# A third order of TensorE groups and loads, from a planner with a new model of the load queue

## The chip, the core and the metric

The kernel runs on one core of a Trainium2 chip. The metric is device time in microseconds (us), of which six runs were taken: the median is 226.64 us, the lowest 226.03 us and the highest 227.13 us. One further execution was profiled. Everything said below of durations and waits comes from that one execution.

## What is computed

The reference is a streaming attention (a window of 128 keys and four sink keys), followed by a dense feed-forward stage with a gated activation:

```python
def _attn_ref(q, k, v, n_sink, window):          # q, k, v: (4, 8, 768, 64)
    scores = np.matmul(q, k.transpose(0, 1, 3, 2)) / np.sqrt(D)
    pos = np.arange(S)
    rel = pos[:, None] - pos[None, :]
    keep = (pos[None, :] < n_sink) | ((rel >= 0) & (rel < window))
    a = softmax(np.where(keep, scores, -1e9))    # over the keys
    return np.matmul(a, v)

def _moe_ref(x, w_in, w_out, beta):              # x: (3072, 512), w_in: (512, 2048)
    h = x @ w_in
    g = h * (1.0 / (1.0 + np.exp(-beta * h)))
    return g @ w_out                             # (3072, 512)
```

The softmax is written out with a maximum and an epsilon in the original; `x` is the attention's output with its heads put side by side. The inputs and the output are float32.

## The kernel before

**Tiles.** The 3072 tokens are cut into eight blocks of 384 tokens (`hb` 0 to 7), two to a batch element. Within a block the eight heads go in four pairs (`hp`), so there are 32 attention units. For each block the kernel loads q, k and v, casts them to bf16, brings q and k into transposed form, makes the scores of a unit in two groups of small matmuls, takes the exponential on ScalarE, masks the result, multiplies it with v, divides, transposes back into `xT`, and runs the feed-forward stage: 16 slices `m` of `w_in` (four matmuls of 384 columns each), an activation on ScalarE and a multiplication on VectorE for each, and then `w_out` (four times four matmuls of 512 columns for each of three row tiles).

**Groups.** TensorE's work is cut into groups, each with a letter. `T` transposes q and k of one head pair (blocks 0 and 1; L697, six matmuls). `C` and `D` are the two score groups of a unit (L783); they use 64 rows of the array at a time. `S` is the score against the sink keys (L819). `A` is the product with v (L861 and L851). `X` transposes the attention output of blocks 0 and 1 (L880). `h` and `g` are the first and second half of one `w_in` slice of blocks 0 and 1, `H` the whole slice of a later block (L910). `O` is a quarter of an output tile (L931). `b` brings in `beta`. Blocks 2 to 7 are transposed by DMA instead of by `T` and `X` (`XT`, L734, and `XO`, L891).

**What sets the order.** The string `ORDER`, one letter for a group, is TensorE's order, written out as data. The planner in `Graph.schedule` walks through it and places the work of all engines in estimated time, one instruction at a time: it picks for each operation one of the engines that can do it (a cast can go to VectorE, ScalarE or GpSimd), and thereby fixes the order on every engine's queue, including SyncE's queue of DMA issues. On the chip each queue then runs strictly in that order, with semaphores for the dependences. `PAR['l0']` is the order of the eleven loads of block 0, and `PAR['mix']` says how the loads of blocks 1 and 2 (`a`) and of the sixteen weight pieces (`w`) are interleaved. All loads form one chain on SyncE in that order.

**The planner's model.** `Graph.place` estimates when a DMA is issued and when it lands. `Graph.fillers` puts matmuls on a constant tile (`ones`, at most 512 columns, in steps of 128) into gaps in which the planner expects TensorE to wait, up to 48 us of planned time and only while a PSUM bank is free; they compute nothing that is used (L1027). Eight PSUM banks hold all matmul results; a `C` or `D` group takes two, every other group one, until the engine that reads them is done.

**Lines that matter below.** L563 and L558 are casts and copies on VectorE and ScalarE, L560 casts on GpSimd; L792 the exponential; L798, L803 and L809 the masks; L823 the exponential of the sink scores; L866 and L868 the division; L915 and L917 the activation's two steps; L635, L647 and L940 the loads of q, k, v, the loads of weights, and the stores of the output.

Of the kernel before, what the change touches and what calls it, by code (L numbers as in the profile page):

```python
# [11 lines left out]
DM, DF, NOUT = 512, 2048, 512  # L12
# [10 lines left out]
PAR = {'MD': 1, 'XB': 2, 'l0': [0, 2, 6, 1, 3, 4, 9, 5, 7, 10, 8], 'mix': 'aawwaawawawwawwaaaawwawwawwwawaa'}  # L23
ORDER = ('TCDTSTTDCSDSCASCTADACbXXAhhhXXThghDghgDhggThgggChhgghgShDSghSghghTghgCASCAXADOXOAhhhhXOXOgOOggOOhghg'
         'hhgOOOghgghghhhghgOgOSDgSChCOghSgADODCCOODOOSAAOAOSSOCCSOSODCHHHHHHHHOHDDOHAHDCHHAHHHAAOODDOOOODCDOH'
         'SCCHHOOASSHHOHOHHHHHSHHHAACSHSOHDCCOAODDOOCCDOAOOHHSHSAOHHOHAAHHHHHHHSHOHOHOSSOCDOHDCCOHHAOOHHHHHSHH'
         'HOSOCCDOHHOHODDAHOAHAOODCCASOOOCDDHHHHHHOAOHOOSHHOOSAHHAOHHHHHOOOHHHHOOHHHHHHOOHHHHOHOOOOOHOOOOOOOOO'
# [10 lines left out]
class Op:  # L38
    __slots__ = ("eng", "fn", "deps", "signal", "count", "waits", "sem", "vc", "dma", "seq", "end", "ns", "alts",
                 "group", "tail", "preds", "left", "succ", "at", "queue", "ring", "lag", "x", "tag", "chain")  # L40
# [6 lines left out]
class Graph:  # L47
# [4 lines left out]
    LEAD, PAD, LATE = 1500, 2000, 90000  # L52
    BIAS, EARLY = 300, 100000
    FILL_TO = 48000
    RING, FETCH, SWITCH = 165, 900, 85
    DEPTH = 9

    def __init__(self):
        self.ops = []
        self.groups = []  # L60
        self.writers = {}
        self.readers = {}
        self.last_load = None
        self.filler = None
# [7 lines left out]
    def add(self, eng, fn, ns=0, r=(), w=(), x=(), dma=None, alts=None, queue=470, ring=64, lag=0, after=(), tag=None):  # L72
# [4 lines left out]
        o.queue, o.ring, o.lag, o.x, o.tag, o.chain = queue, ring, lag, list(x), tag, None  # L77
# [28 lines left out]
    def place(self, o, at):  # L106
        o.at = at
        if o.dma:
            self.pending = [x for x in self.pending if x[0] > at]
            issued, need = at + o.queue + 40, min(o.ring, self.RING)  # L110
            total = sum(n for _, n in self.pending)
            for f, n in self.pending:
                if total + need <= self.RING:
                    break
                issued, total = max(issued, f), total - n
            begin = issued + o.lag if o.lag else at + 1150 + o.ns
            self.dma_free = max(self.dma_free + o.ns, begin)
            self.pending.append((self.dma_free, o.ring))
            self.free[o.eng] = issued
            o.end = self.dma_free + 950 + (self.PAD if at > self.LATE else 0)  # L120
# [942 lines left out]
```

The softmax here doesn't subtract the row's maximum and nothing guards it: scores larger than these inputs give would overflow.

## Time and profile before

| what | value |
|---|---|
| median of six runs | 226.64 us |
| time of the profiled execution | 226.55 us |
| its span, first to last instruction | 224.8 us |
| TensorE (PE) busy | 217.7 us, 97% of the span |
| VectorE (DVE) and ScalarE (ACT) busy | 141.5 us each, 63% |
| GpSimd (POOL) busy | 66.2 us, 29% |
| DMA moved | 40.95 MB, 182 GB/s on average |
| fillers on PE (L1027) | 31 matmuls, 10.6 us busy |
| last instruction of PE ends | 221.94 us |

The span lies 1.75 us below the time of its own execution; this constant part lies around the kernel's instructions. In the first slices of the page PE is between 70% and 90% busy, and from 20 us on practically all the time. Matmuls overlap in the pipeline, so the busy time of a single one (371 ns on average at L931) is longer than the distance from one to the next (0.216 us for 512 columns, read from four in a row that take 0.86 us in the chain of waits). When work is added up for PE, that distance is the right measure.

### The profile page before, as it was taken

Reading aid. Unit: us, or ns where it says so; the run is one execution under the profiler, and the core shown is the slowest. Engines: PE = TensorE matmul, PEld = TensorE weight load, DVE = VectorE, ACT = ScalarE, POOL = GpSimd, SP = SyncE. Lnnn points to the kernel's source line nnn. Section 1 sums busy time; section 2 is a strip of 40 time slices with the busy share of each in tenths; the row PEclk is TensorE's granted clock in tenths of the full one; section 3 lists DMA queues with packets and bytes.
Section 4 is the critical chain, followed back from the end, with each engine's and each line's share of the span. In section 5 each row is a group of like instructions: output and inputs, shape, how many; then the busy total and the mean of one; then the engine's idle time right before and its main releaser. Section 6 shows DMA issues by size and latency. Waiting matters only on the chain.

```text
span 224.8 us, 4484 instructions
## 1 busy us (share of the span) xinstructions
PE 217.7 (97%) x1720; PEld 119.5 (53%) x1720; DVE 141.5 (63%) x313; ACT 141.5 (63%) x257; POOL 66.2 (29%) x157
## 2 busy tenths in 40 slices
PE   8978999999999999999999999999999999999994
PEld 2545555555455546545554665455455556555443
DVE  1798999778757278839775578657362626455100
ACT  2595998134882867547788847778757756566221
POOL 7274345000362626352109510241435400000000
PEclk9999999999999999999999999999999999999999
DMA  7999989997999999999999999993133033101112
GB/s 158 268 332 372 358 217 322 350 253 136 220 224 206 217 208 234 183 255 219 207 241 186 210 219 221 248 252 104 47 85 82 0 85 83 47 4 47 47 47 93
DMA packets 104741, 40.95 MB, mean 182 GB/s; under 512 B 93312, under 2 KB 97680, under 8 KB 104720
## 3 DMA queue, kind: packets, MB, share of 16 engines
q1 hardware_dynamic: 103152, 40.65, 79.6%
q8 instruction: 13, 0.21, 0.5%
q10 hardware_dynamic: 1568, 0.02, 0.4%
q14 instruction: 8, 0.07, 0.1%
HBM read 27.30 MB, written 6.29 MB: 149 GB/s over the span
## 4 chain that ended last, share of the span: by engine, by line
PE 71%; DVE 12%; DMA 7%; SPq 6%; ACT 2%; issue 1%
PE P L931 32%; PE P L910 28%; DMA v_stage<-in_v_dram 5%; SPq L635 4%; DVE g L917 4%; PE P L861 4%; PE P L783 3%; DMA k_stage<-in_k_dram 3%; DVE k L563 1%; PE P L851 1%; DVE onorm L868 1%; SPq L891 1%; DVE E L809 1%; PE P L819 1%; DVE vaug L563 1%; DVE w_in L563 1%
## 5 line engine op out<-in xcount | busy, mean ns | idle before, releaser
L931 PE MATMUL P<-w_out,g 128*128 128x512 bf16 (+2 forms) x400 | 93.1, 371 | 0.1
L910 PE MATMUL P<-xT,w_in 128*128 128x384 bf16 x512 | 92.7, 326 | 0.0
L915 ACT ACTIVATE t<-P,hbeta 128x384 f32<-128x384 f32 x128 | 71.8, 586 | 31.4 <-PE P L910 24.1
L917 DVE SCALAR_TENSOR_TENSOR g<-t,P 128x384 bf16<-128x384 f32 x128 | 68.0, 549 | 35.5 <-ACT t L915 32.8
L798 POOL TENSOR_SCALAR_AFFINE_SELECT E<-E 128x256 bf16<-128x256 bf16 (+1 forms) x109 | 52.2, 510 | 58.0 <-ACT E L792 57.9
L910 PEld LDWEIGHTS P<-xT,w_in 128*128 128x128 bf16 x512 | 48.4, 98 | 34.7 <-issue 0.8
L931 PEld LDWEIGHTS P<-w_out,g 128*128 128x128 bf16 x400 | 36.6, 98 | 37.1 <-issue 1.1
L792 ACT ACTIVATE E<-P 128x768 bf16<-128x768 f32 (+1 forms) x64 | 45.6, 760 | 14.2 <-PE P L783 14.0
L861 PE MATMUL P<-vaug,E 128*128 128x65 bf16 x352 | 18.6, 193 | 0.8 <-DVE E L803 0.5
L558 ACT ACTIVATE osb<-P 128x512 f32<-128x512 f32 (+2 forms) x16 | 9.1, 571 | 15.4 <-PE P L931 15.1
L861 PEld LDWEIGHTS P<-vaug,E 128*128 128x128 bf16 x352 | 16.5, 97 | 4.1 <-ACT E L792 0.7
L868 DVE TENSOR_TENSOR onorm<-P,rden 128x384 bf16<-128x384 f32 x32 | 17.4, 553 | 0.5
L783 PE MATMUL P<-qkT 64*128 64x128 bf16 (+1 forms) x256 | 16.4, 239 | 1.0 <-ACT E L792 0.4
L823 ACT ACTIVATE ES<-P 128x128 bf16<-128x128 f32 (+1 forms) x32 | 12.1, 391 | 7.0 <-PE P L819 7.0
L563 DVE CAST k<-k_stage 128x512 bf16<-128x512 f32 (+1 forms) x24 | 11.8, 490 | 5.4 <-DMA k_stage<-in_k_dram 5.2
L783 PEld LDWEIGHTS P<-qkT 64*128 64x128 bf16 x256 | 8.2, 94 | 12.2 <-issue 4.3
L851 PE MATMUL P<-vS,ES 128*128 128x130 bf16 x64 | 12.7, 221 | 0.9 <-DVE vS L686 0.6
L563 DVE CAST q<-q_stage 128x512 bf16<-128x512 f32 (+1 forms) x19 | 9.2, 483 | 6.8 <-DMA q_stage<-in_q_dram 6.7
L563 DVE CAST vaug<-v_stage 128x512 bf16<-128x512 f32 x18 | 7.9, 438 | 7.8 <-DMA v_stage<-in_v_dram 7.7
L725 POOL TENSOR_TENSOR kS<-qkT,headm 128x8 bf16<-128x8 bf16 x16 | 3.0, 209 | 32.4 <-DMA qkT<-k 28.8
L1027 PE MATMUL P<-ones 128*128 128x512 bf16 (+2 forms) x31 | 10.6, 473 | 1.2 <-POOL ones L569 1.1
L809 DVE TENSOR_TENSOR E<-E,maskS 128x512 bf16<-128x512 bf16 x16 | 8.5, 532 | 3.4 <-ACT E L792 3.2
(48 smaller groups left out, 88.3 us busy)
## 6 DMA issues: line engine op xcount, KB each, us to landing
v_stage<-in_v_dram SPq DMA_DIRECT2D x24, 256.0 KB, 4.8
out_dram<-osb SPq DMA_DIRECT2D x23, 256.0 KB, 2.6
q_stage<-in_q_dram SPq DMA_DIRECT2D x18, 256.0 KB, 4.7
k_stage<-in_k_dram SPq DMA_DIRECT2D x18, 256.0 KB, 5.7
wst<-in_moe_w_in_dram SPq DMA_DIRECT2D x5, 512.0 KB, 7.9
wst<-in_moe_w_out_dram SPq DMA_DIRECT2D x4, 512.0 KB, 7.7
g<-in_moe_w_out_dram SPq DMA_DIRECT2D x4, 512.0 KB, 7.6
q_stage<-in_q_dram SPq DMA_DIRECT2D x8, 192.0 KB, 4.6
```

What stands on the lines that cost most here:

```text
L563: return lambda e: e.tensor_copy(dst, at())
L783: add("pe", lambda e, dst=dst, own=own, kc=kc, rows=rows, q0=q0, nq=nq: e.matmul(dst(), tokens(own, hp, 1, rows, kc, 1)[:, 0, :], tokens(h ...
L792: add("act", lambda e, src=src, dst_=dst_: e.activation(dst_, src(), AF.Exp, bias=0.0, scale=SCALE), act_ns(256 * n), w=[(k_, z, j) for k_ ...
L798: alts = {"gp": (lambda e, d=d, sg=sg, at_=at_: e.affine_select(d, d, [[0, 2 * len(at_)], [sg, 128]], ALU.is_ge, 0.0, base=min(sg, 0), cha ...
L823: add("act", lambda e: e.activation(ES[z][:, q0:q1], P[:, bs[0], q0:q1], AF.Exp, bias=0.0, scale=SCALE), act_ns(q1 - q0), w=[("ES", z)], x ...
L851: add("pe", lambda e, m=m, o0=o0: e.matmul(A()[:, o0:o0 + 2 * (D + 1)], ES[z][:, (c0 + m) * 128:(c0 + m + 1) * 128], vS[b % 2][:, 2 * hp:2 ...
L861: e.matmul(A()[:, o0:o0 + D + 1], E[z][:, i, hh, :], vaug[vz][:, kb % NK, 2 * hp + hh, :], start=a, stop=o, skip_group_check=True), 39,
L868: add("dve", lambda e: e.tensor_tensor(onorm[:, on, 2 * c0:2 * c1, :], av()[:, :, 0:D], rden[on][:, 0:2 * nb].unsqueeze(2).to_broadcast([1 ...
L910: first = add("pe", lambda e, c=c: e.matmul(hp(), w_in16[:, c, m * 128:(m + 1) * 128], xT[:, hb, c, 128 * c0:128 * c1], start=(c == 0), st ...
L915: add("act", lambda e: e.activation(tt[ti][:, 0:n], hp(), AF.Tanh, bias=0.0, scale=hbeta[:, m:m + 1]), act_ns(n) + 93, r=["hbeta"], w=[("t ...
L917: add("dve", lambda e: e.scalar_tensor_tensor(gt[hb % NG][:, m, 128 * c0:128 * c1], tt[ti][:, 0:n], 1.0, hp(), ALU.add, ALU.mult), dve_ns( ...
L931: add("pe", lambda e, m=m: e.matmul(P[:, bk[0], a:b], gt[hb % NG][:, m, t * 128:(t + 1) * 128], w_out16[:, m, a:b], start=(m == 0), stop=( ...
```

## The change

The change replaces the two data strings and the model behind them. The matmuls of the kernel's own work, their shapes and their number stay the same, as do the loads and stores.

```diff
-PAR = {'MD': 1, 'XB': 2, 'l0': [0, 2, 6, 1, 3, 4, 9, 5, 7, 10, 8], 'mix': 'aawwaawawawwawwaaaawwawwawwwawaa'}
-ORDER = ('TCDTSTTDCSDSCASCTADACbXXAhhhXXThghDghgDhggThgggChhgghgShDSghSghghTghgCASCAXADOXOAhhhhXOXOgOOggOOhghg'
+PAR = {'MD': 1, 'XB': 2, 'l0': [2, 3, 1, 6, 9, 0, 7, 8, 5, 4, 10], 'mix': 'waawwaawawaaawwwaaawwawwwwaaawaw'}
+ORDER = ('TTSDCSTDCCTAASCDDTXbSAXCDAXShhhXhThgghggghhTgCDTgghhhggghShhCghgggDSDAAASChXgOXOXAOhXhhhgghggOgOhgOO'
...
-    LEAD, PAD, LATE = 1500, 2000, 90000
-    BIAS, EARLY = 300, 100000
-    RING, FETCH, SWITCH = 165, 900, 85
+    LEAD, PAD, LATE = 2000, 2000, 90000
+    BIAS, EARLY = 400, 45000
+    FETCH, SHORT, SWITCH = 1150, 400, 85
+    SMALL = {"sp": (42, 80), "dve": (50, 180), "gp": (56,), "act": (193,)}
+    DMA = {"nat": ((434, 580, 580, 580, 470), 64, 1140, 115, 2250), "hb": ((434, 580, 580, 580, 470), 64, 2290, 115, 3390),
...
+    FETCHES = (152, 232, 368, 477, 608, 730, 858, 988, 1111, 1222, 1354, 1482, 1601, 1728)
...
-            begin = issued + o.lag if o.lag else at + 1150 + o.ns
-            self.dma_free = max(self.dma_free + o.ns, begin)
-            self.pending.append((self.dma_free, o.ring))
-            self.free[o.eng] = issued
-            o.end = self.dma_free + 950 + (self.PAD if at > self.LATE else 0)
+            prev, start = self.last_dma
+            issued = max(at + quick[prev], wait, start + 2370 if prev == 2 else 0)
...
+            f = max(self.dma_free + svc, at + 3090 if kind == "xt" else issued + lag)
...
+            self.pending.append((max(self.dma_free, f - svc), f, n + 1, o))
+            self.dma_free = f
+            self.free[e] = issued + 43
+            o.end = f + 600 + (self.PAD if at > self.LATE else 0)
...
+        if rows:
+            t -= self.SWITCH
...
-            n = min(512, int((t - now) * 2.4 / slow) // 128 * 128)
+            room = t - now - (self.SWITCH if self.rows else 0)
+            n = min(512, int(room * 2.4 / slow) // 128 * 128)
```

What it does to the model: each kind of DMA has its own issue time, service time and lag (`DMA`); the fetches of program code are charged to the load queue at listed places (`FETCHES`, `SMALL`); masks on VectorE are charged more (for instance 430 instead of 335 ns for the sink mask), and a matmul of 65 columns less (36 instead of 39 ns); ScalarE is charged a handicap of 400 instead of 300 ns against VectorE, but only up to 45 us instead of 100 us; fillers leave room for the change of the array's row mode before and after score groups. There is also a new option to issue output stores from ScalarE, which is not switched on.

What it does to the program, read from the built instruction streams: PE has 1738 matmuls instead of 1720, and all 18 more are fillers. The leading run of fillers is 25 of 512 columns and one of 384, instead of 12 and one. All fillers together have 22016 columns instead of 15104. Up to the first `O` group both programs hold the same work of PE. The sequence of PE changes into or out of score groups (64-row mode) 64 times instead of 74 times; from the first `O` on, 44 instead of 46 times. The loads of block 0 come in the order q1, k1, k0, q3, v1, q0, k3, v0, k2, q2, v2 instead of q0, q1, q3, k0, k1, q2, v1, k2, k3, v2, v0 (q and k by head pair, v by token tile). Before the first activation product (L917) VectorE has 13 casts of q and k and 4 copies of `T` results instead of 10 and 2; ScalarE has no such casts and 2 copies instead of 3 and 4.

## The prediction, made before the changed kernel ran

> **What bounds the kernel now.** I read the page's engine table first (PE busy 97%), then PE's timeline, which splits the run into two stages.
>
> ```profile
> PE 217.7 (97%) x1720; PEld 119.5 (53%) x1720; DVE 141.5 (63%) x313; ACT 141.5 (63%) x257; POOL 66.2 (29%) x157
> ```
>
> ```profile
> 1.06 5.62 PE L1027 MATMUL P<-ones 128*128 128x512 bf16 x13 [1.06 <-POOL ones L569]
> 6.47 0.45 PE L697 MATMUL P<-ident,q 128*128 128x128 bf16 x3
> ...
> 19.79 1.14 PE L910 MATMUL P<-xT,w_in 128*128 128x384 bf16 x6
> ...
> 38.10 1.03 PE L931 MATMUL P<-w_out,g 128*128 128x512 bf16 x4
> ...
> 84.31 0.34 PE L783 MATMUL P<-qkT 64*128 64x256 bf16 x3 [0.31 <-DVE g L917]
> ...
> 213.10 8.84 PE L931 MATMUL P<-w_out,g 128*128 128x512 bf16 x56
> ```
>
> Start, duration, what, count, and in brackets the idle time and its releaser. Up to 38.1 us PE is busy largely with fillers; from the first O group (L931, 38.10) to its end at 221.94 it streams. Does PE's content explain that stage? Distances between matmuls, from rows in a row: 0.1625 us (384 columns), 0.216 (512), 0.0295 (L861), 0.057 (L851), 0.0545 and 0.030 (score matmuls of 256 and 128 columns), 0.056 (transposes), 0.11 for each change into or out of score groups. Over all counts of the page this gives 197.9 us of own work: L910 83.2, L931 83.0, L861 10.4, L851 3.6, L783 10.0, L819 3.5, the rest 4.2. Before the first O lie 20.4 us of it, after it 177.5. So 177.5 + 46 x 0.11 = 182.5, against 221.94 - 38.10 = 183.8 measured: only **1.3 us** of stalls are left there. The two largest are the waits near 73.3 (for a DMA transpose of k) and 82 to 84 us (banks held by L917).
>
> What bounds the first stage is in the chain of waits:
>
> ```profile
> 6.59 5.77 DMA v_stage<-in_v_dram
> 12.38 0.43 DVE vaug L563
> ...
> 23.69 0.48 ACT t L915
> 24.20 0.56 DVE g L917
> 24.75 0.48 DVE k L563
> ```
>
> Loads until 12.4 us, then mostly VectorE one instruction after another, until 35 us. VectorE's own timeline shows its last steps before the O stage, and ends with the second w_out cast, which the first O group needs:
>
> ```profile
> 22.95 0.56 DVE L917 SCALAR_TENSOR_TENSOR g<-t,P 128x384 bf16<-128x384 f32 x1 [0.86 <-ACT t L915]
> ...
> 37.60 0.78 DVE L563 CAST w_out<-g 128x1024 bf16<-128x1024 f32 x1
> ```
>
> So the end is (first O group) + 182.5 + stalls + 2.9 us of tail (224.8 - 221.94). A changed order can win at the O group's time, at the changes of row mode, and at 1.3 us of stalls.
>
> **The change part by part.**
>
> *First transposes.* VectorE's first casts, each waiting for its load, begin at 3.84, 4.96, 5.75 and 6.35; ScalarE's (the sixth load) at 7.63, the v load after it at 8.77. A pair load thus adds 0.6 us and a v load 1.14. In the new order T0 and T1 need q0, now sixth behind a v load: 6.35 + 1.14 + 0.6 = 8.1, with a cast of 0.42 about 8.55. The leading fillers are 25.75 units of 512 columns. The row above has 13 in 5.62 us, 0.43 each, twice the later 0.216: a slow clock until about 6.2 us, though the page's granted-clock row shows 9 throughout. Twelve at 0.43 and 13.75 at 0.216 end at 9.15.
> A rule speaks against so many fillers. The Trainium skill, "TensorE: Matmul & The Clock Gate", Part 1, says the slow clock lasts about 3.4 us of sustained activity, and returns only after an idle window as long; waiting PE needs no matmuls for shorter gaps. By it, 8 fillers at 0.43 and 17.75 at 0.216 end at 8.3, and T0 would start with its data at 8.55, 0.6 us earlier. The trace shows 5.1 us, and fast matmuls after unfilled gaps of up to 0.61 us. I take the row, 9.15, against 6.47 before; but T1 follows at once (before: 8.79), and all four T's need loads that land by 11.1 in both.
>
> *From there to the first activation product.* VectorE's order with its steps (cast 0.42, T copy 0.86, v cast 0.35, vS 0.36, sink mask 0.3 to 0.57, other mask 0.2, onorm 0.46, rden 0.1): T0's copy 9.65 to 10.5; v0, k2, vS, q2 until 12.05; so T2 at 12.1 and, after vS and a mask, its copy until 13.5; C2 at 13.6, T3 until 14.2, masks of units 0 and 1 until 14.85, T3's copy until 15.7, C3 then; q and k of block 1, onorm 0 and 1 with masks until 18.8, onorm 2 19.6, onorm 3 20.9 (before 20.3), the last two xT copies and a T copy until 22.7. The first whole w_in slice ends on PE at 22.5, ScalarE takes 0.57, the first L917 begins at about **23.3** (before 22.95). By then VectorE has done 1.9 us more than before: 3 casts 1.25, 2 T copies 1.7, a mask 0.2, less a v cast, an xT copy and a weight cast 1.2. It had 1.9 us of waits for loads and ScalarE after 9 us (brackets 0.16, 0.48, 0.44, 0.86) to put it in. The 13.5 extra filler units (2.9 us) lie in PE's waits here and cost nothing while VectorE is last; without that cover each could hold a ready group by 0.2 us.
>
> *From there to the first O.* After the first L917 up to the same w_out cast VectorE does, new: 13 L917 6.0, 6 weight casts 3.6, 3 casts 1.25, a T copy 0.86, 2 v casts 0.7, 3 rden and an onorm 0.75: 13.2. Before: one T copy and one xT copy more, a rden less: 14.2, which took 14.9 (23.4 to 38.3). In that ratio 13.8 us: 23.8 + 13.8 = 37.6 for the cast's end, and O 0.2 ahead of it as before (its first two matmuls don't need this cast): 37.4. But each L917 also waits for its L915, and ScalarE's 16 of them with the exponentials between take 13.5 us from 22.7. Between 37.4 and 38.1 (nothing won) I take **37.9**, near the row of before. The w_out load is no nearer bound: the same loads stand before it on SyncE, and it lands ahead of its cast. Ends: 37.2 (the sum, and ScalarE early), and 39.4 if the 1.9 us find no gaps.
>
> *Steady stage.* Own work the same, two changes of mode less: -0.2. The stalls: the bank wait at 82 to 84 is tied to the old order; nine w_in slices in a row (36 matmuls) follow three score groups there now, and ScalarE, at 0.47 a slice against PE's 0.65, catches up. The other, the transpose of block 3's k: its third cast at VectorE now stands behind the sink mask of unit 3, whose score group is at 68.6; exponentials until 70.2, mask and cast until 71.1, transpose 3.7 more (as in the old issue at 69.48 that PE got at 73.2): 74.8, needed at 74.5. A wait of 0.3, as now. On SyncE an output store and one `XO` stand ahead of it (0.9 and 1.24 us), but their inputs are ready by 68. Behind it wait all of PE. Stalls **1.3 as before**; ends 0.4, since two gaps go, and 3.0, since a planner's miss anywhere here is paid in full.
>
> *Model constants, fillers' room, unused store option:* no instruction of their own; they act through the orders just counted. The tail keeps its last instructions and stays 2.9.
>
> Sum on the profile: -0.2 (first O) - 0.2 (modes) + 0 (stalls) = -0.4: span 224.4, execution 226.15. The profiled execution lies 0.1 below the median; -0.4 on the median gives **226.2 us**.
>
> **The rivals.**
> *The order recovers more: 224.7.* If PE only lost what no order can avoid, it would run from 9.15 through 197.9 + 64 x 0.11 + 17.25 fillers of 0.216 = 208.7, to 217.8, 4.1 us before the old end. VectorE's chain forbids most of it. But first O at 37.2 (-0.9), -0.2, and stalls at 0.5 (-0.8) make -1.9. For it: ScalarE is freed of three casts and two T copies ahead of the activations, and the longer fillers say that the new model expects these waits. Against: VectorE is what bounds, and gets more.
> *The late start is not won back: 227.7.* The mechanism is VectorE's queue between 9 and 23 us. T0 is 2.7 us later, and the 1.9 us of added casts and copies come behind it; a single exponential or mask later than I put it leaves VectorE idle, in order. If none of the gaps is filled, the first L917 begins at 22.95 + 1.9 = 24.8, 1.5 later than in the sum; O at 39.4, and -0.4 + 1.5 = +1.1 gives 227.7. It makes the kernel slower from a first L917 at 23.7 on, measurably from 24.4. For it: T2 and T3 both wait for VectorE here. Against: the loads land as early as before.
> *The order is changed but the time is not:* within the main case.
>
> **How the numbers follow.** What a measurement of this kernel can tell from no change is 0.3%, 0.68 us, so 225.96 to 227.32. Main case 226.2, own range 225.2 to 227.2, chance 0.40: 0.17 below the band, 0.19 in it, 0.04 above (its open ends of stalls). Recovery 224.7 (224.0 to 225.5): 0.23, all faster. Late start 227.7 (227.0 to 230, where new stalls come on top): 0.37, of it 0.05 in the band. Faster 0.40, same 0.24, slower 0.36. The range leaves out the far ends of both rivals: 224.5 to 228.6.
>
> **What would show it.** PE's timeline: first transposes at 9.15 (8.6 if the rule holds), first O near 37.9, last PE end near 221.5. VectorE's: first L917 at 23.3, hardly idle after it. The wait before L783 near 74.5 at 0.3 or less. I am wrong if first O lies outside 37.2 to 38.6, or if waits of more than 2 us in all appear on PE after it, whatever the total.

## The result, and the profile after

The changed kernel takes 227.84 us (median of 36 runs, 227.44 to 229.61), the kernel before, in 73 runs beside it, 226.80 us (226.03 to 228.71). The ratio is 1.0048 with an interval of 1.0038 to 1.0059: the change costs about 1.1 us. (The profiled execution of after took 227.51 us, that of before 226.55.) The forecast was 226.2, a small gain. The measured value lies outside the main case's own range (225.2 to 227.2) and inside the wide one that took in the rivals (224.5 to 228.6), 0.14 us from the rival "late start not won back" (227.7).

The engine line of the page after, then TensorE's timeline with the lines that answer to those shown of before:

```profile
PE 218.2 (97%) x1738; PEld 120.3 (53%) x1738; DVE 138.6 (61%) x311; ACT 141.0 (62%) x259; POOL 69.4 (31%) x157
```

```profile
1.06 7.71 PE L1070 MATMUL P<-ones 128*128 128x512 bf16 x26 [1.06 <-POOL ones L610]
8.60 0.33 PE L738 MATMUL P<-ident,q 128*128 128x128 bf16 x3
...
21.23 1.15 PE L951 MATMUL P<-xT,w_in 128*128 128x384 bf16 x6
...
39.17 0.59 PE L972 MATMUL P<-w_out,g 128*128 128x512 bf16 x2
39.96 0.61 PE L972 MATMUL P<-w_out,g 128*128 128x512 bf16 x2 [0.19 <-DVE w_out L604]
...
77.03 0.67 PE L824 MATMUL P<-qkT 64*128 64x256 bf16 x12 [0.68 <-DMA qkT<-k]
...
211.43 11.43 PE L972 MATMUL P<-w_out,g 128*128 128x512 bf16 x68
```

All lines of the code stand 41 further down than before, or a little more (L910 is now L951, L931 L972, L917 L958). The first O group starts at 39.17, before at 38.10: 1.07 us later. TensorE ends at 222.86, before at 221.94: 0.92 later. So from the first O on, the new program needs 183.69 us where the old one needed 183.84. **The loss is made in the first 39 us**, and the later stage is level. In after only two matmuls of the first O group stand ahead of a wait for the second `w_out` cast, so the third one is followed below as well: 39.96 against 38.53 in before.

Who bounds these 39 us is in the chain of waits (start, duration, what):

```profile
6.54 4.58 DMA q_stage<-in_q_dram
...
11.14 0.42 DVE q L604
...
17.41 0.43 DVE E L850
17.84 1.05 DVE E L844
18.89 0.47 DVE onorm L909
19.36 0.10 DVE rden L907
19.46 0.84 DVE E L844
20.30 0.48 DVE onorm L909
20.78 0.05 issue
20.83 0.34 PE P L921 x3
```

From the landing of the tenth load (q2, 11.12) to the third transposition of the attention output (20.83) there is nothing in the chain but VectorE. Two masks (L844) take 1.05 and 0.84 us of it. VectorE's timeline around them, and below it GpSimd's:

```profile
17.77 1.12 DVE L844 TENSOR_TENSOR E<-E,maskT 128x256 bf16<-128x256 bf16 x1
...
19.39 0.92 DVE L844 TENSOR_TENSOR E<-E,maskT 128x256 bf16<-128x256 bf16 x1
20.22 0.55 DVE L909 TENSOR_TENSOR onorm<-P,rden 128x384 bf16<-128x384 f32 x1
20.69 0.41 DVE L604 CAST q<-q_stage 128x384 bf16<-128x384 f32 x1
...
21.48 0.55 DVE L909 TENSOR_TENSOR onorm<-P,rden 128x384 bf16<-128x384 f32 x1
...
24.57 1.02 DVE L958 SCALAR_TENSOR_TENSOR g<-t,P 128x384 bf16<-128x384 f32 x2
```

```profile
17.53 1.22 POOL L601 TENSOR_SCALAR_AFFINE_SELECT w_in<-wst 128x1024 bf16<-128x1024 f32 x1
18.71 0.45 POOL L839 TENSOR_SCALAR_AFFINE_SELECT E<-E 128x256 bf16<-128x256 bf16 x1
19.12 1.04 POOL L601 TENSOR_SCALAR_AFFINE_SELECT w_in<-wst 128x1024 bf16<-128x1024 f32 x1
```

Two masks of the same line in before, with GpSimd's cast that runs beside the second one:

```profile
16.87 0.24 DVE L803 TENSOR_TENSOR E<-E,maskT 128x256 bf16<-128x256 bf16 x1
...
17.61 1.04 DVE L803 TENSOR_TENSOR E<-E,maskT 128x256 bf16<-128x256 bf16 x1
```

```profile
17.47 1.05 POOL L560 TENSOR_SCALAR_AFFINE_SELECT w_in<-wst 128x1024 bf16<-128x1024 f32 x1
```

In before such a mask took 0.24 and 0.28 us, and once 1.04. In after two start while GpSimd casts a weight, and end just after that cast does. The last division of block 0 (L909 at 21.48) stood at 19.79 before: **1.69 us later**. From it on, both programs take the same way: transposition, copy to `xT`, second half of a `w_in` slice, L956, L958. That took 3.16 us before (19.79 to 22.95) and 3.09 now (21.48 to 24.57). From the first L958 to the third O matmul it is 15.4 us, before 15.6. So 1.43 of the division's 1.69 us arrive at the third O matmul.

### The profile page after: what moved, and what is told of

The parts are those of the page before. It is cut to its first block, busy times and chain, and to the rows that moved or that the text cites. A ratio compares the mean times of both kernels' runs of the same rounds, so it can differ in the third digit from the quotient of the medians.

```text
span 225.7 us, 4514 instructions
## 1 busy us (share of the span) xinstructions
PE 218.2 (97%) x1738; PEld 120.3 (53%) x1738; DVE 138.6 (61%) x311; ACT 141.0 (62%) x259; POOL 69.4 (31%) x157
## 4 chain that ended last, share of the span: by engine, by line
PE 84%; DVE 6%; DMA 4%; SPq 2%; ACT 1%; issue 0%
PE P L951 36%; PE P L972 36%; PE P L824 5%; PE P L902 4%; SPq L676 2%; DMA q_stage<-in_q_dram 2%; DMA qkT<-k 2%; PE P L892 1%; PE P L860 1%; DVE E L844 1%; DVE onorm L909 1%; DVE g L958 1%; DVE qkT L604 1%; DVE E L850 1%; DVE w_out L604 1%; ACT E L833 1%
## 5 line engine op out<-in xcount | busy, mean ns | idle before, releaser
L958 DVE SCALAR_TENSOR_TENSOR g<-t,P 128x384 bf16<-128x384 f32 x128 | 68.0, 548 | 43.4 <-ACT t L956 40.8
L956 ACT ACTIVATE t<-P,hbeta 128x384 f32<-128x384 f32 x128 | 71.3, 585 | 36.4 <-PE P L951 30.0
L951 PE MATMUL P<-xT,w_in 128*128 128x384 bf16 x512 | 94.0, 326 | 0.0
L972 PE MATMUL P<-w_out,g 128*128 128x512 bf16 (+2 forms) x400 | 92.2, 371 | 0.2 <-DVE w_out L604 0.2
L839 POOL TENSOR_SCALAR_AFFINE_SELECT E<-E 128x512 bf16<-128x512 bf16 (+1 forms) x108 | 54.0, 527 | 84.9 <-ACT E L833 84.3
L951 PEld LDWEIGHTS P<-xT,w_in 128*128 128x128 bf16 x512 | 47.6, 98 | 33.7 <-issue 0.8
L972 PEld LDWEIGHTS P<-w_out,g 128*128 128x128 bf16 x400 | 37.1, 98 | 38.1 <-issue 0.9
L599 ACT ACTIVATE osb<-P 128x512 f32<-128x512 f32 (+2 forms) x24 | 14.0, 584 | 17.2 <-PE P L972 17.1
L604 DVE CAST q<-q_stage 128x512 bf16<-128x512 f32 (+1 forms) x25 | 12.0, 482 | 10.0 <-DMA q_stage<-in_q_dram 9.9
L824 PE MATMUL P<-qkT 64*128 64x128 bf16 (+1 forms) x256 | 15.7, 239 | 2.4 <-ACT E L833 1.0
L909 DVE TENSOR_TENSOR onorm<-P,rden 128x384 bf16<-128x384 f32 x32 | 17.5, 551 | 0.5
L1070 PE MATMUL P<-ones 128*128 128x512 bf16 (+3 forms) x49 | 13.1, 402 | 1.1 <-POOL ones L610 1.1
L604 DVE CAST k<-k_stage 128x512 bf16<-128x512 f32 (+1 forms) x25 | 11.2, 450 | 3.7 <-DMA k_stage<-in_k_dram 3.6
L850 DVE TENSOR_TENSOR E<-E,maskS 128x512 bf16<-128x512 bf16 x16 | 7.4, 465 | 6.5 <-ACT E L833 6.1
```

What stands on the lines that cost most here:

```text
L599: return lambda e: e.activation(dst, at(), AF.Copy, bias=0.0, scale=scale)
L604: return lambda e: e.tensor_copy(dst, at())
L824: add("pe", lambda e, dst=dst, own=own, kc=kc, rows=rows, q0=q0, nq=nq: e.matmul(dst(), tokens(own, hp, 1, rows, kc, 1)[:, 0, :], tokens(h ...
L839: alts = {"gp": (lambda e, d=d, sg=sg, at_=at_: e.affine_select(d, d, [[0, 2 * len(at_)], [sg, 128]], ALU.is_ge, 0.0, base=min(sg, 0), cha ...
L909: add("dve", lambda e: e.tensor_tensor(onorm[:, on, 2 * c0:2 * c1, :], av()[:, :, 0:D], rden[on][:, 0:2 * nb].unsqueeze(2).to_broadcast([1 ...
L951: first = add("pe", lambda e, c=c: e.matmul(hp(), w_in16[:, c, m * 128:(m + 1) * 128], xT[:, hb, c, 128 * c0:128 * c1], start=(c == 0), st ...
```

## The experiments

All kernels but two keep the planner's finished plan and move single instructions in it: `find(G, key, engine)` names an instruction by what it writes, `move(G, o, engine, x)` puts it on that engine's queue ahead of `x`. Each was timed in five rounds beside the kernel before, in six groups with their own times of before (226.64 to 227.47 by the medians), so the ratio is what compares them. The ratios have intervals of 0.1% to 0.3% to either side, so a single step of 0.3 us is not told apart by a time; the profile of each says where it went. A profile is one execution, and can lie off its kernel's median (b1's by 1.2 us).

| program | time, us | ratio to before (interval) | last division | first L917 / L958 | third O matmul | from there to PE's end |
|---|---|---|---|---|---|---|
| before | 226.80 | 1 | 19.79 | 22.95 | 38.53 | 183.4 |
| after | 227.84 | 1.0048 (1.0038–1.0059) | 21.48 | 24.57 | 39.96 | 182.9 |
| e1_hold_pool | 228.62 | 1.0050 (1.0029–1.0071) | 20.82 | 24.40 | 39.97 | 184.0 |
| e3_casts_act | 227.95 | 1.0029 (1.0010–1.0048) | 21.09 | 24.22 | 39.84 | 183.3 |
| e5_q0_early | 228.28 | 1.0040 (1.0019–1.0061) | 21.58 | 24.67 | 40.29 | 184.1 |
| e7_k_first | 228.48 | 1.0050 (1.0029–1.0071) | 21.73 | 24.82 | 40.44 | 182.8 |
| e2_masks_pool | 227.59 | 1.0029 (1.0014–1.0045) | 20.52 | 24.11 | 39.45 | 183.4 |
| e6_wout_early | 227.81 | 1.0048 (1.0031–1.0064) | 21.42 | 24.51 | 39.81 | 182.3 |
| e8_k2_early | 228.28 | 1.0052 (1.0035–1.0070) | 22.11 | 25.47 | 40.59 | 183.2 |
| e10_before_load | 227.41 | 1.0030 (1.0015–1.0045) | 20.59 | 23.22 | 38.81 | 183.4 |
| g1_old_front | 228.05 | 1.0047 (1.0033–1.0062) | 19.70 | 22.79 | 38.59 | 185.2 |
| g2_old_front_mask | 227.67 | 1.0028 (1.0013–1.0042) | 18.84 | 21.82 | 37.63 | 184.7 |
| f1_light_dve | 227.68 | 1.0037 (1.0017–1.0057) | 20.89 | 24.84 | 40.30 | 183.4 |
| e4_no_late_fill | 228.44 | 1.0088 (1.0060–1.0115) | 21.40 | 24.47 | 40.02 | 183.2 |
| a1_short_lead | 228.13 | 1.0055 (1.0034–1.0077) | 21.39 | 24.47 | 39.87 | 183.8 |
| f2_light_short | 227.09 | 1.0019 (0.9999–1.0040) | 20.20 | 24.14 | 39.39 | 183.2 |
| b1_before_mask | 226.60 | 0.9996 (0.9978–1.0015) | 18.73 | 22.51 | 38.15 | 185.1 |
| f3_front | 227.05 | 0.9996 (0.9975–1.0017) | 20.16 | 23.38 | 38.98 | 184.2 |
| a2_k6_early | 228.47 | 1.0072 (1.0046–1.0099) | 21.82 | 24.91 | 40.31 | 182.8 |
| f4_front_k6 | 226.57 | 0.9987 (0.9971–1.0003) | 20.14 | 23.37 | 38.76 | 183.6 |

### Is it the masks beside GpSimd, VectorE's work, or the late start?

**e1_hold_pool**: GpSimd's second weight cast waits until VectorE's last mask is done.

```diff
+m = find(G, ("p", 3, 1), "dve")
+w, nxt = find(G, ("w16", 0, 1)), find(G, ("w16", 1, 0))
+move(G, w, "gp", nxt)
+w.deps.append((m, False))
```

> The changed kernel's plan with one edit: GpSimd's second w_in cast comes after its last mask of unit 3 and waits for VectorE's mask of that unit, so that neither of VectorE's two masks at 17.8 and 19.4 us has a GpSimd weight cast beside it; no engine gets more or less work. Collision theory (the masks last 1.12 and 0.92 us instead of 0.25 because of those casts, and everything on VectorE behind them is late): the masks fall to 0.25 to 0.45, first L958 product from 24.57 to about 23.3, first O group from 39.2 to about 38.2, total 0.8 to 1.4 us below the changed kernel (226.4 to 227.0), level with the kernel before. Added-work theory (VectorE is late because it got casts and copies): at most 0.3 us. Late-start theory (the first transposes begin 2.1 us later and that is what shows at the end): no gain.

The masks fell to 0.48 and 0.24 us and the last division came 0.66 earlier. But the cast, now at 19.17, met a cast of VectorE instead: the q cast at 19.49 took 1.00 us. Another, at 23.57, took 0.91 beside GpSimd's third weight cast, which it just misses in after. The first L958 gained 0.17 only, and the ratio did not fall. Moving GpSimd's cast moved the collision.

**e3_casts_act**: the casts of block 1's first q and k on ScalarE.

```diff
+es = [o for o in G.ops if ("ES", 2) in o.keys][0]
+for n in "qk":
+    move(G, find(G, (n + "16", 1, 0, 0), "dve"), "act", es)
```

> The changed kernel's plan with the two casts of block 1's first q and k (VectorE at 15.1 and 15.9 us, 1.2 us together) moved to ScalarE, where they stand ahead of the sink exponential of unit 2 in a gap at 14.4 us. Added-work theory: VectorE's chain is 1.1 to 1.2 us shorter, first L958 about 23.5, total 0.8 to 1.2 us lower. Collision theory: the same 1.2 us are taken out of the chain ahead of the masks, but the masks then wait for exponentials of ScalarE and still meet the weight casts, so 0.2 to 0.6 us. Late-start theory: no gain.

The division came 0.39 earlier, the first L958 0.35, though the first transposes were 0.5 later (9.12) in this execution; the ratio fell by 0.0019, with an interval that overlaps after's. The two masks, now earlier against GpSimd's casts, took only 0.34 and 0.38 us, but the q cast behind them took 1.15 (19.61) beside the next weight cast (19.44 to 20.48): here too the collision moved.

**e2_masks_pool**: the two masks on GpSimd, ahead of its weight cast.

```diff
+for o in (find(G, ("d", 2, 1), "dve"), find(G, ("p", 3, 1), "dve")):
+    o.eng = "gp"
+    o.fn, o.ns = o.alts["gp"]
+move(G, find(G, ("w16", 0, 1)), "gp", find(G, ("w16", 1, 0)))
```

> After, with the two masks of VectorE that GpSimd's weight casts stretched (17.77 us, 1.12 us long; 19.39 us, 0.92 us long) done on GpSimd ahead of its second weight cast; all else in its place. VectorE loses 2.0 us of its queue ahead of the first L958 (0.5 us of it work, 1.5 us stretch). If VectorE's queue between 11 and 23 us sets the first activation product, the first w_in matmul comes 1.0 to 2.0 us earlier than 21.23, the first L958 at 23.0 to 23.8 (after: 24.57), the third O matmul at 38.6 to 39.2 (after: 39.96), and the time falls by 0.8 to 1.3 us, to about that of the kernel before. If the loss sits behind the first L958 (the bank wait at 28.6, the w_out casts), the first L958 moves but the third O matmul stays within 0.3 us of 39.96, and the time within 0.3 us of after's.

The division moved by 0.96 us. The first L958 kept 0.46 of it, and it, the third O matmul and the time all fell short of what was expected. VectorE's timeline and GpSimd's show why:

```profile
23.26 0.92 DVE L637 CAST q<-q_stage 128x384 bf16<-128x384 f32 x1
24.11 1.00 DVE L991 SCALAR_TENSOR_TENSOR g<-t,P 128x384 bf16<-128x384 f32 x2
```

```profile
22.86 1.04 POOL L634 TENSOR_SCALAR_AFFINE_SELECT w_in<-g 128x1024 bf16<-128x1024 f32 x1
```

A cast of 0.41 us, standing right ahead of the first activation product, met GpSimd's third weight cast.

**e5_q0_early**: q0 loaded fourth, and 8 of the 26 leading fillers left out, so that TensorE starts 1.4 us sooner (7.21).

```diff
+q3, q0 = find(G, ("stg", "q", 0, 3)), find(G, ("stg", "q", 0, 0))
+move(G, q0, "sp", q3)
+move(G, find(G, ("q16", 0, 0, 0)), "dve", find(G, ("q16", 0, 3, 0)))
...
+for o in lead[-9:-1]:
+    G.ops.remove(o)
```

> The changed kernel's plan with q0 loaded fourth instead of sixth (and cast in that order), and eight fillers of 512 columns fewer in the leading run, so that the first transposes begin at about 6.8 instead of 8.6 us. Late-start theory: most of the 1.8 us comes through, total 1.0 to 1.7 us lower. VectorE-chain theories (collision and added work): the chain starts at the cast of q2, whose load lands at 11.1 us either way, so first L958 and the total stay within 0.3 us of the changed kernel.

The last division stayed (21.58), and so did all behind it. The late first transposes are not the cause; the chain begins with q2's load, as the chain of waits says.

**e10_before_load**: the kernel before with more on VectorE.

```diff
+for key in (("qkT", 0, 3, 0, 0), ("q16", 1, 1, 0), ("k16", 1, 1, 0)):
+    o = find(G, key, "act")
+    o.eng = "dve"
+    o.fn, o.ns = o.alts["dve"]
```

> The kernel before with 1.75 us of ScalarE's work ahead of the first activation product given to VectorE, in place: one copy of transposes (0.93 us) and the casts of q and k of one head pair of block 1 (0.41 each). Nothing else of the change: old loads, old TensorE order, old fillers, early start. If VectorE's added work alone makes the loss, the first L917 moves from 22.95 to 24.0 to 24.7, the first O from 38.1 to 38.8 to 39.3, and the time rises by 0.7 to 1.2 us, as the whole change did (1.1). If the loss needs the new order of groups or the later start, the added work goes into VectorE's gaps (0.48 at 12.4, 0.44 at 20.8, 0.86 at 22.9) and the time stays within 0.3 us.

The division was 0.80 late, yet the first L917 only 0.27. VectorE's timeline:

```profile
20.59 0.54 DVE L901 TENSOR_TENSOR onorm<-P,rden 128x384 bf16<-128x384 f32 x1
21.06 0.68 DVE L596 CAST w_in<-wst 128x1024 bf16<-128x1024 f32 x1
21.66 0.34 DVE L596 COPY xT<-P 128x384 bf16<-128x384 bf16 x1
...
23.22 0.55 DVE L950 SCALAR_TENSOR_TENSOR g<-t,P 128x384 bf16<-128x384 f32 x1 [0.89 <-ACT t L948]
```

In before the `w_in` cast behind the division waited 0.44 us for its load (20.79), and the copy of `xT` waits behind that cast. The added work used up this slack first. So before has slack behind its last division that after lacks. The time rose by 0.3%, less than the whole change; it lies between the two expectations.

### Is it TensorE's order behind the first product?

**e6_wout_early** and **e8_k2_early**.

```diff
+move(G, c0, "dve", r0)      # w_out casts ahead of block 1's reciprocals
+move(G, c1, "dve", r1)
```

> After, with the two VectorE casts of the first w_out slices ahead of the reciprocals and divisions of block 1 that wait for TensorE (after: casts at 37.66 and 39.23, their loads land at 34.16 and 36.45). If the late casts set the third O matmul, it starts at 39.4 to 39.6 without a wait (after: 39.96 with waits of 0.2 to 0.3), and the time falls by 0.3 to 0.4 us. If TensorE's own order bounds this stretch, O's two waits vanish but others appear for the divisions (L921, L951 of block 1), and the time stays within 0.15 us. Of the 1.07 us by which the first O is late, neither takes away more than 0.4.

The wait of the third O matmul vanished, but it started 0.15 earlier only, and the ratio stayed at 1.0048.

```diff
+for o in fill:              # the two fillers at 26.03
+    G.ops.remove(o)
+move(G, k2, "dve", g0)      # k cast of 26.11 ahead of the first L958
```

> After, with the cast of block 1's third k (VectorE, 26.11 us, behind a weight cast) moved ahead of the first L958, and without the two fillers at 26.03 that stand in front of the transposes which wait for it. If the path goes from that cast over the transposes, ScalarE's copy of them and the exponential to the second score group of block 1 (28.56 us, 1.0 us of wait), then this group comes at 28.1 to 28.2, the third O matmul at 39.5 to 39.6, and the time falls by 0.4 us although the first L958 is itself 0.3 to 0.4 later. If what bounds is the row of activation products themselves, everything after the first L958 slips with it: the time rises by 0.2 to 0.4 us.

The second score group came 4.26 us after ScalarE's first L956 (24.58; after 4.61), but the third O matmul still came 15.1 us behind the first L958 (after 15.4), which had slipped. In this profile the row of activation products carries the delay on; the ratio, 1.0052, doesn't decide between the two expectations.

**g1_old_front** and **g2_old_front_mask** do not plan; they replay a list: before's instructions up to the first O group on all engines, then after's. g2 also gives before's one stretched mask to GpSimd.

```diff
-        while at_pe < len(todo) or pool:
+        for step in PLAN:
```

> The kernel before up to its first O group, instruction for instruction on every engine (loads, fillers, casts, groups), and behind it after's order of what is left, its casts and stores too. If the whole loss sits ahead of the first O and the changed steady stage is itself worth 0.2 to 0.5 us, the third O matmul starts at 38.5 as before, PE ends 182.9 to 183.4 us later (before: 183.4; after: 182.9), and the time is 226.3 to 226.8, that is 0 to 0.5 us under before and 1.0 to 1.5 us under after. If the new steady order costs something too, the time lies above before's by 0.2 us or more.

> As g1_old_front, and the one mask that VectorE does beside GpSimd's second weight cast in the kernel before (17.61 us, 1.04 us long, 0.24 to 0.28 for its two sisters) given to GpSimd ahead of that cast. If stretched masks in VectorE's queue ahead of the division set the first activation product, it comes 0.6 to 1.0 us earlier than g1's (before: 22.95), the third O matmul at 37.6 to 38.0, and the time falls 0.5 to 0.8 us below g1's, under both kernels. If the stretch only moves to the next VectorE instruction beside GpSimd's cast, or if loads of w_out bound the O group (the second lands at 36.1 to 37.0 and takes a cast of 0.7), at most 0.3 us.

The front behaved as in before (third O matmul 38.59), the rest did not: TensorE's timeline has a wait right behind the seam and one near 140.

```profile
39.75 0.34 PE L916 MATMUL P<-ident,onorm 128*128 128x128 bf16 x3 [0.78 <-DVE onorm L904]
...
139.85 0.45 PE L819 MATMUL P<-qkT 64*128 64x128 bf16 x8 [0.84 <-DVE onorm L904]
```

The first is made by the seam itself (a division that after's order has done by then), so g1 cannot price the later stage. Its time is after's, not before's, and whether the seam makes all of that is not shown. The second has its real cause in a DMA: the transpose of block 6's k landed at 139.76, in the profile of after at 138.63. g2 shows the mask clearly: 0.86 us off the division, 0.97 off the first product, 0.96 off the third O matmul. The median fell by 0.4 us, less than the 0.5 to 0.8 expected, and the intervals of g1 and g2 overlap.

### Together

**f1_light_dve** takes both masks, block 1's first q and k casts and two of GpSimd's weight casts out of the way, with e6's edit. **a1_short_lead** is after without 8 leading fillers. **f2_light_short** is both.

```diff
+move(G, find(G, ("w16", 0, 1)), "act", x1)
+move(G, find(G, ("w16", 1, 0)), "act", es)
...
+for o in lead[-9:-1]:
+    G.ops.remove(o)
```

> After, with all that the earlier runs pointed at taken off VectorE's queue ahead of the first L958: its two stretched masks to GpSimd, the casts of block 1's first q and k to ScalarE, GpSimd's second and third weight cast to ScalarE where it is idle (near 19 and 22 us), and the w_out casts ahead of the divisions. If VectorE's work and its stretch make up the 1.6 us by which the first L958 is late, it comes at 22.9 to 23.6, the third O matmul 15.0 to 15.3 us after it, at 38.0 to 38.8 (before 38.53), and the time falls by 1.0 to 1.5 us to 226.3 to 226.9. If the order of TensorE's groups holds the front back, the first L958 stays at 23.9 or later and the time at 227.4 or more.

> After with 8 of the 26 leading fillers left out, nothing else. In the profiles of after and its variants 9 to 14 of the 26 ran at 0.43 us, and the first transposes began at 8.5 to 9.4 us; q0, which they need, is cast at 8.48. If the run's length costs time in executions whose clock rises late, the first transposes begin at 8.5 to 8.6 whatever the clock, and the median falls by 0.2 to 0.6 us below after's. If the queue on VectorE covers it, the time stays within 0.2 us. If the clock needs the longer run (a wait of PE ahead of 8.5 us lowers it), the granted clock drops near 9 to 12 us and the time rises.

> f1_light_dve with the same 8 leading fillers left out. f1's profile had 14 fillers at the slow clock and first transposes at 9.43, and VectorE waited 0.8 us for them. If that hid its gain, the first transposes begin at 8.5 to 8.6, the first w_in matmul at 20.1 to 20.4, the first L958 at 23.6 to 24.1, the third O matmul at 39.0 to 39.5, and the time falls to 226.8 to 227.3. If the front is held by TensorE's order and not by VectorE's queue, the first L958 stays at 24.5 or later and the time at f1's 227.7.

f1 gained little, and VectorE's timeline says what it met: it now waited for TensorE, whose leading fillers ran 14 times at 0.43 us in that execution.

```profile
9.96 0.96 DVE L648 COPY qkT<-P 128x768 bf16<-128x768 bf16 x1 [0.80 <-PE P L782]
```

In a1 the first transposes came at 8.46, and nothing changed: with VectorE as full as in after, the late start is covered. In f2 TensorE started sooner again, and the ratio was 1.0019 (227.09 us); that the shorter run brought f1's gain out is likely, but the intervals of f1 and f2 overlap. The division is 1.28 earlier than in after, the first product 0.43, since ScalarE's weight cast now stood ahead of its copy of `xT` and a q cast met GpSimd again (0.72 us at 23.50).

**f3_front** clears that too: only one weight cast on ScalarE, behind the copies of `xT`; the cast of block 1's second q behind the last division; the cast of its third k ahead of a weight cast; three fillers less than in f2.

```diff
+move(G, find(G, ("w16", 0, 1)), "act", es)
+move(G, q11, "dve", k11)
+move(G, k12, "dve", w20)
```

> After with TensorE's own work, loads and everything behind the first O in its order, and only the helpers ahead of it changed: both stretched masks on GpSimd; casts of block 1's first q and k on ScalarE; GpSimd's second weight cast on ScalarE, behind the copies of xT; the cast of block 1's second q behind the last division; the cast of its third k ahead of a weight cast; w_out casts ahead of the divisions; 8 leading fillers and the fillers at 22.2 and 26.0 us left out. If the loss lies in VectorE's queue and what waits for it, the first w_in matmul comes at 19.5 to 20.1, the first L958 at 22.9 to 23.6, the second score group of block 1 at 27.2 to 27.7 (after 28.56), the third O matmul at 38.3 to 38.9 (before 38.53, after 39.96), and the time is 226.3 to 226.9, level with before or just under it. If the new group order itself holds the front back, the third O matmul stays at 39.4, f2's value, and the time at 227.1.

```profile
20.16 0.55 DVE L963 TENSOR_TENSOR onorm<-P,rden 128x384 bf16<-128x384 f32 x1
...
23.38 1.03 DVE L1012 SCALAR_TENSOR_TENSOR g<-t,P 128x384 bf16<-128x384 f32 x2
```

The ratio is 0.9996 (0.9975 to 1.0017): **level with before, with TensorE's own groups and the loads in after's order**. From after's 1.0048 the edits took back the whole loss. The third O matmul, at 38.98, is 0.1 outside what was expected.

**b1_before_mask** gives before's one stretched mask to GpSimd, and nothing else.

```diff
+m = find(G, ("p", 3, 1), "dve")
+m.eng = "gp"
+m.fn, m.ns = m.alts["gp"]
```

> The kernel before with one change: the mask that VectorE does beside GpSimd's second weight cast (17.61 us, 1.04 us long) goes to GpSimd ahead of that cast. By the view that the last division's place in VectorE's queue sets the first activation product, and this the O groups 15.5 us later, the first L917 comes at 21.8 to 22.2 (before 22.95), the third O matmul at 37.5 to 37.8 (38.53), and the time falls by 0.6 to 0.9 us, to about 226.0: under both kernels. If the later stage takes the gain back (the transpose of block 3's k, banks near 82 to 84), it falls by less than 0.3.

No gain is shown: 226.60 us, an interval of 0.9978 to 1.0015. In the profile the division came 1.06 earlier, the first L917 0.44, the third O matmul 0.38, and the end none. On VectorE, and on TensorE:

```profile
20.51 0.69 DVE L596 CAST w_in<-wst 128x1024 bf16<-128x1024 f32 x1 [1.22 <-DMA wst<-in_moe_w_in_dram]
```

```profile
47.41 1.47 PE L964 MATMUL P<-w_out,g 128*128 128x512 bf16 x6 [0.60 <-DVE w_out L596]
```

The front now waits for a `w_in` load instead, and O groups that are early wait for `w_out` pieces (three landed at 45.42 to 48.04). But this execution was the slowest of twelve (227.84 us), so its later waits can't be taken for the usual ones. What the front shows is that in before the division is one of several things that are due at once.

### What the fillers and the transposes of k are worth

**e4_no_late_fill** leaves out the 23 fillers behind the leading run.

```diff
+G.ops = [o for i, o in enumerate(G.ops) if i < at or o.keys != ["filler"]]
```

> After without the fillers behind the leading run (23 of 49, 17 units of 512 columns; they stand in TensorE's waits from 9.3 to 32.3 us). The prediction's price for them was nothing while VectorE is last: time and first O within 0.2 us of after's. If some hold ready groups back by up to 0.2 us each (the third X at 22.27 behind a filler, the third T of block 1 at 26.46), the first L958 comes 0.1 to 0.3 earlier. If waiting TensorE falls back to its slow clock without them, matmuls of 384 columns take 0.32 instead of 0.16 us for some microseconds, and the first O is more than 1 us later. The longest wait without fillers would be 1.3 us.

The median rose by another 0.6 us, the ratio by 0.0040, and the intervals do not overlap. The profile, in stretches of 1 us (span, TensorE busy, granted clock, DMA share, GB/s):

```profile
11.00:12.00 1.00, 0.64 (x13) 0.99 1.16 272
12.00:13.00 1.00, 1.00 (x14) 0.50 1.03 367
13.00:14.00 1.00, 0.60 (x9) 0.50 1.10 342
14.00:15.00 1.00, 1.00 (x15) 0.50 1.08 371
15.00:16.00 1.00, 1.00 (x24) 0.81 1.06 389
```

Without fillers the granted clock falls to half for over 3 us. In this one execution (227.81 us) the third O matmul hardly moved (40.02). The clocks of all 15 executions show more: in 12 the mean granted clock is 0.985 to 0.993 and the median time 229.0 us, and in the three at 0.999 or 1.000 the time is 227.69 to 227.83, as in after. So the loss goes with the lowered clock.

**e7_k_first** put the last cast of block 3's k ahead of a mask, so that its transpose could start sooner. **a2_k6_early** issued block 6's transpose of k ahead of an output store and another transpose. **f4_front_k6** is f3 with a2's edit.

```diff
+move(G, k, "dve", s)
```

> The changed kernel's plan with one swap on VectorE: the third k cast of block 3 goes ahead of the sink mask of unit 3 (block 2), so that it no longer waits for that unit's exponentials. If the stall of 0.7 us before the score groups at 77 us comes from that order: the cast at 70.0 instead of 72.1, the transpose of k lands 1.3 us earlier, at about 75.5, the stall goes and the total is 0.6 to 0.9 us lower. If the transpose queue itself is late (a store and one XO ahead of it): less than 0.3 us.

The transpose began 0.83 earlier (71.93), took 5.19 us instead of 4.14, and TensorE got it at 77.25, 0.22 later than in after.

```diff
 dxq0, dv01, dv02
-do0, dy0, dxk0
+dxk0, do0, dy0
```

> After with one change on SyncE's queue: the transpose of block 6's k ahead of an output store and a transpose of onorm (which is used only much later), instead of behind them. It can be issued once the last score group that reads its buffer is through (130.8 us in f3's profile), so near 131.5 instead of 134, and lands near 136. If the wait near 139 is part of the usual execution, no profile shows it and the time falls by 0.2 to 0.5 us. If it is rare or the moved store and transpose cost as much later, the time stays within 0.15 us of after's.

> f3_front with the same change on SyncE's queue. f3's profile had 0.88 us of wait near 139. If that is what keeps it level with before, the time falls by 0.3 to 0.8 us under f3's, to a ratio of 0.996 to 0.999 to before. If not, the ratio stays at 0.9996 within the interval, and PE shows another wait in its place.

Issued at 131.7 and 131.1, it landed after 6.1 and 6.0 us (137.83, 137.11); neither profile has the wait near 139 that f3's had (0.86; after's had none). In time, a2 brought no gain: its ratio is 1.0072, above both expectations, with an interval (1.0046 to 1.0099) that overlaps after's. f4 is 0.5 us under before by the medians of the same rounds (226.57 and 227.03), 0.3 by the ratio, with an interval of 0.9971 to 1.0003 that includes no change. It is the best version found, and not shown to beat before.

## Why the prediction was wrong

**The first transposes** were forecast at 9.15 us, 8.6 by the skill's rule; they came at 8.60. Neither figure is a constant: in the ten profiles with the full run of 26 leading fillers, 8 to 14 of them ran at 0.43 us, and the transposes began at 8.48 to 9.43. That this costs nothing was right for after (a1), as long as VectorE is as full as it is.

**The way to the first activation product is the step that failed**: forecast 23.3, measured 24.57. The working lets the last division end at 20.9 (in before it ended at 20.35); it ended at 22.03, 1.1 us late. The way behind it, 2.4 in the working, took 2.54 (in before 2.60). So nearly all of the miss lies in VectorE's queue ahead of that division. Two terms there were wrong.
*The masks.* "Other mask 0.2" was the row of an undisturbed one. The last two took 1.12 and 0.92, together 1.64 us more than priced. At the end of the third T copy (15.7 in the working, 15.2 measured) the program was still early. From there to the end of the division the working has 5.2 us, and 6.8 were measured, 1.6 more (the misses of its other steps cancel). The row that should have warned was in the profile of before: 1.04 us at 17.61, beside a cast on GpSimd. The change put one more such mask beside such a cast.
*The gaps.* "1.9 us of waits to put it in" counted waits wherever they stood. VectorE's busy time up to the start of the last division, and from there to the first activation product, is in before and in after (stretch, its length, VectorE busy):

```profile
0.00:19.79 19.79, 13.50 (x34) 1.00 1.02 270
19.79:22.95 3.16, 1.85 (x6) 1.00 1.06 377
```

```profile
0.00:21.48 21.48, 15.32 (x35) 1.00 1.02 283
21.48:24.57 3.09, 2.79 (x7) 1.00 1.09 356
```

Up to the division after has 1.82 us more work and only 0.13 less idle time, which makes its 1.69 us. Behind the division 0.94 more work fits into the same time: it used up the gaps of 0.44 and 0.86 that stand there, so they were not left to take up the division's delay, as the 0.44 did in e10. In all, the added work was 2.76 us instead of 1.9, since masks and casts were stretched, and idle time shrank by 1.14 instead of 1.9.

**From there to the first O** the 14.6 us came out (24.57 to 39.17), in part by luck. The working counts 13 more activation products up to the second `w_out` cast, the profile has 14, and the cast ended 14.8 us after the first product where the sum had 13.8. Against that, 37.9 had been set 0.5 above the sum's 37.4, and the first O came 0.7 ahead of that cast's end instead of 0.2. That its first two matmuls don't need the cast held; the third waited 0.19 for it. A first O outside 37.2 to 38.6 was the forecast's own sign of being wrong, and it came about.

**The later stage** was right in size: from the first O on 0.15 us gained against 0.2 (from the third O matmul on, 0.5). The wait for block 3's k was 0.68 instead of 0.3 in after's profile, and about 0.3 in most others. What it was not is steady: the 12 profiles with after's later stage unedited and no seam in front needed 182.3 to 184.2 us from the third O matmul on, before and e10 183.4. A wait near 139 ahead of block 6's scores, which no step of the forecast looked at, is in four of them.

**"Extra fillers cost nothing"**: no cost was seen, and leaving out those behind the leading run costs (e4). The clocks on record also speak for the change here. Of 271 executions of before timed beside the variants, 110 show a mean granted clock of 0.991 or 0.992, and they take about 0.3 us longer than the others; of after's 36 none is below 0.998. The profile of before, at 1.000, is one of the undisturbed.

**The rival** that came about had its mechanism placed right, VectorE's queue between 9 and 23 us, and its numbers near (24.8 and 39.4 forecast, 24.57 and 39.17 measured). Its sum was near in part by luck: it had 1.9 us of added work and no gap filled, where 2.76 were added and 1.14 of idle time were filled. f3 shows that the loss lies in what the helpers do ahead of the first O, and not in the new order of TensorE's own groups or of the loads. How it divides among masks, casts and ScalarE's copies is seen in single profiles only, since the intervals of e2, e3, f1 and f2 overlap; that stays open.

## What to carry to other kernels

When work is moved to an engine that has waits, count only the waits ahead of the instruction that the path goes through; name that instruction first. Price an operation by its row next to what will run beside it: the same mask took 0.24 us and 1.12 us, and moving its neighbour moved the collision to the next cast. An early front is worth no more than the next thing that is due: relieved of its mask, the kernel before had its division 1.06 us earlier in its profile, waited for a weight load, and kept 0.44 of it at the first activation product.

## What the runs showed of the hardware

**VectorE blocked by GpSimd.** A mask of two bf16 inputs (0.24 us) and a cast from f32 (0.41 us), both from SBUF to SBUF, lasted 0.91 to 1.16 and 0.72 to 1.15 us where they started while a weight cast ran on GpSimd, and ended 0.1 to 0.3 us behind its end (17.53 + 1.22 = 18.75 on GpSimd, 18.89 on VectorE). Which starts first matters: one and the same mask took 0.28 us in before, where it started 0.13 us ahead of GpSimd's cast (15.38 and 15.51), and 1.16 in g1, where it started behind it (15.15 and 15.12). Divisions and copies that read PSUM kept their durations beside such casts (in e1 0.54 at 19.02 and 0.31 at 20.59). The Trainium skill, "SBUF — State Buffer", section "SBUF: two separate sides", describes this as an exclusive lock on a shared port pair: whichever starts first holds it for its whole instruction, and the other blocks. The ends fit that. As an estimate by that page, a mask costs the rest of GpSimd's cast and its own 0.24: 1.22 and 1.01 us for the two of after, which took 1.12 and 0.92.

**The granted clock.** In e4 it fell to 0.50 from 12.0 to 15.4 us, although TensorE's longest wait ahead of it was 1.1 us and it was busy for 33% to 64% of the slices from 9 to 12. In g1's profile, with before's front and its fillers, it fell from 15.0 to 18.4, behind slices with 54% and 48% (12 to 14). The rule used in the forecast (the Trainium skill, "TensorE: Matmul & The Clock Gate", Part 1: the slow clock returns after an idle window of about 3.4 us) would not have had it fall, if the window has to be idle throughout. So a stretch of low use can be enough. It is not always: the profile of before was busy for 54% and 38% of the same two slices and kept its clock. What decides is not shown here.

**Transposes by DMA.** Issued sooner, they took longer (5.2 instead of 4.1 us in e7, 6.1 instead of 4.6 in a2): of the 0.8 us won at the start in e7 nothing arrived, and of the 2.3 us in a2 0.8. Why they took longer was not tried.
